# Dense products beside a column-tiled run, issued as four 128x32 column tiles

## The chip, the cores and the metric

The kernel runs on one core of one Trainium2 chip. The metric is the device time of one execution in microseconds. Matrix products run on TensorE (PE in the profile; its weight loads are PEld), the other work on VectorE (DVE), ScalarE (ACT) and GpSimd (POOL), and SyncE (SP) issues the transfers.

## The reference

One transformer block over 2048 tokens of width 1024: an attention with a memory that is carried over four segments of 512 tokens, with 32 heads of 32, and a gated feed-forward layer of width 3584. Cut to what matters:

```
h  = x + A(layernorm(x))        h2 = h + B(layernorm(h))

A: q, k, v = x @ wq, x @ wk, x @ wv          # heads of 32, 4 segments of 512
   for s in range(4):
       p     = softmax(qs @ ks.T * 32**-0.5 + causal mask)
       a_dot = p @ vs
       a_mem = (phi(qs) @ M) / (phi(qs) @ z + 1e-6)     # phi(t) = t+1 if t>0 else exp(t)
       o     = sigmoid(beta) * a_mem + (1 - sigmoid(beta)) * a_dot
       M, z  = M + phi(ks).T @ vs, z + sum(phi(ks))
   return o @ wo
B: return (silu(x @ w1) * (x @ w3)) @ w2
```

Weights and activations are bf16.

## The kernel before

Every piece of work is made into an operation of a graph (`Op`), with its engine, the buffers it reads and writes, the PSUM banks of its group, and a function `emit` that issues its instructions later. The order on each engine is not searched for: the table `ORDER` lists, for each of the five engines, the numbers of the operations in sequence, `BANKS` gives the PSUM bank of each group, and `HOLD` adds some waits between transfers and matmuls. `schedule` puts the operations in that order; its own model of times only decides the order in which the program is written down and which DMA semaphore is used. `Graph.emit` then walks through the operations, puts the waits on semaphores ahead of each, and calls its `emit`; the last instruction of an operation signals.

TensorE is used in four shapes, and each of its operations has a `mode`:

- "full", 128 rows by 128 columns: all dense products (the q, k, v projections, `wo`, and the feed-forward layer), made by `mms` (line 707 issues them), and the first transposes (line 719). `mms` cuts the eight products of a PSUM group into operations of four matmuls each, every one with its own weights of 128x128 and 512 moving columns.
- "row", 32 by 128: the scores of attention (line 1079), four heads at once in four row tiles, into banks 0 to 3.
- "col", 128 by 32: numerators and denominators of attention (`finish`, lines 1165 and 1172) and the memory's products (`products`, line 1000), four heads at once in four column tiles, each tile with weights of 32 columns.
- "tile", 32 by 32: the reading of the memory (line 1296).

There are eight half segments of attention, 0 to 370 us. In each, ten score operations alternate with dense operations that come from other parts of the model (projections of the next segment, `wo` of an earlier one, or the feed-forward layer), so that ScalarE has time for the exponentials. Then a column run follows: numerators, denominators, memory products. Ahead of it and behind it stand dense runs. After the last one the feed-forward layer is left, dense throughout.

## Time and profile before

| | |
|---|---|
| median of 3 runs (lowest to highest) | 884.22 us (883.82 to 886.32) |
| span of the profiled execution | 882.6 us (its time with what lies around the span is not given apart) |
| TensorE busy | 877.7 us, 5821 matmuls |
| weight loads | 398.1 us, 5821 |
| VectorE, ScalarE, GpSimd busy | 439.5, 301.7, 162.9 us |
| dense products of 512 columns (line 707), by the page's groups | 896 + 896 for w1 and w3, 952 for w2, 256 for wo, the rest projections |
| 128x32 matmuls of line 1172 and of line 1000 | 896 and 384 |
| granted TensorE clock | 1.000 |
| instruction packets of TensorE's queue | 46 |

How to read it: busy times of PE are unions of pipelined matmuls whose ends are modelled, so a matmul of 512 columns is listed with 379 ns although the next one starts sooner. The starts in the timeline are what counts. The forms read rows*columns of the array, then partitions x moving elements: 128*32 128x512 is one column tile. A window row lists, for each engine, busy time and count of instructions, then the granted clock, the DMA share and GB/s.

### The profile page before, as it was taken

The page shows a single profiled execution, that of the slowest core. Times are in us where ns is not written, and L with a number is a line of the kernel's source. Part 1 is how long each engine was busy: PE and PEld are TensorE (multiplying, and loading weights), DVE is VectorE, ACT ScalarE, POOL GpSimd, SP SyncE. Part 2 cuts the span into 40 slices and gives each one's busy share as a digit, 9 for nine tenths or more (in the row PEclk, how much of TensorE's full clock was granted, in tenths as well). Part 3 has the DMA queues.
Part 4 walks back from the last instruction along what each step waited for, and adds up shares of the span by engine and source line. Part 5 has one row for each costly group of instructions (what it writes and reads, how often), then busy time and mean ns, then how long its engine had stood idle before and what let it go on. Part 6 is the DMA issues. An engine that isn't in the chain of part 4 may idle for free.

```text
span 882.6 us, 13741 instructions
## 1 busy us (share of the span) xinstructions
PE 877.7 (99%) x5821; PEld 398.1 (45%) x5821; DVE 439.5 (50%) x735; ACT 301.7 (34%) x345; POOL 162.9 (18%) x226
## 2 busy tenths in 40 slices
PE   8999999999999999999999999999999999999998
PEld 5443444444444444444444444444444444444445
DVE  5787878876666777745354301322243344231011
ACT  5878675768656655511111000111011111110000
POOL 1534344335242444303000000000000000000000
PEclk9999999999999999999999999999999999999999
DMA  7989938555962627395483411211322322201011
GB/s 227 214 185 215 251 85 225 144 144 161 233 158 82 168 68 172 93 283 160 113 242 95 113 36 30 78 54 54 96 76 62 96 72 61 89 7 48 19 42 42
DMA packets 148956, 105.75 MB, mean 120 GB/s; under 512 B 46368, under 2 KB 134688, under 8 KB 147872
## 3 DMA queue, kind: packets, MB, share of 16 engines
q1 hardware_dynamic: 148896, 104.89, 45.8%
q8 instruction: 46, 0.75, 0.4%
q14 instruction: 14, 0.11, 0.0%
HBM read 84.94 MB, written 9.44 MB: 107 GB/s over the span
## 4 chain that ended last, share of the span: by engine, by line
PE 99%; DMA 1%; SPq 0%; issue 0%; DVE 0%; DVEq 0%
PE ps L707 92%; PE ps L1079 3%; PE ps L1172 3%; DMA wp<-in_A_wk_dram 1%; PE ps L1000 0%; PE ps L1296 0%; SPq L388 0%; PE ps L1165 0%; PE ps L719 0%; DVE ob L1401 0%; DVEq L524 0%
## 5 line engine op out<-in xcount | busy, mean ns | idle before, releaser
L707 PE MATMUL ps<-hnT,w1b 128*128 128x512 bf16 x896 | 216.2, 379 | 0.0
L707 PE MATMUL ps<-hnT,w3b 128*128 128x512 bf16 x896 | 213.9, 379 | 0.0
L707 PE MATMUL ps<-w2b,hm 128*128 128x512 bf16 (+2 forms) x952 | 199.2, 366 | 0.0
L1369 ACT ACTIVATE sg<-ps 128x512 bf16<-128x512 f32 x112 | 66.8, 597 | 385.5 <-PE ps L707 384.3
L1372 DVE SCALAR_TENSOR_TENSOR t<-sg,ps 128x512 bf16<-128x512 bf16 x112 | 76.6, 685 | 190.1 <-ACT sg L1369 189.8
L1093 ACT ACTIVATE et<-ps 128x2048 bf16<-128x2048 f32 x80 | 150.1, 1876 | 47.7 <-PE ps L1079 45.8
L707 PEld LDWEIGHTS ps<-w2b,hm 128*128 128x128 bf16 x952 | 90.9, 98 | 103.2 <-issue 0.3
L707 PEld LDWEIGHTS ps<-hnT,w1b 128*128 128x128 bf16 x896 | 86.3, 98 | 105.6 <-issue 5.6
L707 PEld LDWEIGHTS ps<-hnT,w3b 128*128 128x128 bf16 x896 | 86.4, 98 | 105.3 <-issue 3.1
L1102 POOL TENSOR_SCALAR_AFFINE_SELECT et<-et 128x512 bf16<-128x512 bf16 (+1 forms) x96 | 83.1, 877 | 112.5 <-ACT et L1093 112.5
L1377 DVE SCALAR_TENSOR_TENSOR hm<-t,ps 128x512 bf16<-128x512 bf16 x112 | 76.2, 684 | 42.5 <-PE ps L707 40.6
L1401 DVE TENSOR_TENSOR ob<-hr,ps 128x512 bf16<-128x512 bf16 (+2 forms) x34 | 21.9, 654 | 122.4 <-PE ps L707 122.3
L707 PE MATMUL ps<-xnT,wp 128*128 128x512 bf16 (+1 forms) x352 | 60.9, 321 | 1.1 <-DMA wp<-in_A_wk_dram 1.1
L707 PE MATMUL ps<-wo,oT 128*128 128x512 bf16 x256 | 61.1, 380 | 0.0
L707 PE MATMUL ps<-hnT,wp 128*128 128x512 bf16 x256 | 59.7, 380 | 0.0
L1118 DVE TENSOR_TENSOR sum<-sum,et 128x512 bf16<-128x512 bf16 (+1 forms) x64 | 40.5, 640 | 6.1 <-POOL et L1102 3.8
L707 PEld LDWEIGHTS ps<-xnT,wp 128*128 128x128 bf16 x352 | 27.9, 98 | 27.3 <-issue 3.5
L707 PEld LDWEIGHTS ps<-wo,oT 128*128 128x128 bf16 x256 | 23.8, 98 | 29.7 <-issue 3.0
L707 PEld LDWEIGHTS ps<-hnT,wp 128*128 128x128 bf16 x256 | 23.6, 98 | 29.7 <-issue 3.7
L1079 PE MATMUL ps<-qT,kT 32*128 32x128 bf16 (+3 forms) x512 | 31.7, 301 | 0.0
L1341 DVE TENSOR_TENSOR h<-h,ps 128x512 bf16<-128x512 bf16 x32 | 21.6, 679 | 20.2 <-PE ps L707 19.8
L707 PE MATMUL ps<-wp,hnT 128*128 128x512 bf16 x128 | 30.4, 380 | 0.0
(101 smaller groups left out, 568.2 us busy)
## 6 DMA issues: line engine op xcount, KB each, us to landing
w1b<-in_B_w_dram SPq DMA_DIRECT2D x28, 512.0 KB, 4.1
w3b<-in_B_w_dram SPq DMA_DIRECT2D x28, 512.0 KB, 4.4
wp<-in_A_wv_dram SPq DMA_DIRECT2D x8, 1024.0 KB, 5.9
wp<-in_A_wq_dram SPq DMA_DIRECT2D x7, 1024.0 KB, 6.2
wp<-in_A_wk_dram SPq DMA_DIRECT2D x7, 1024.0 KB, 7.6
w2b<-in_B_w_dram SPq DMA_DIRECT2D x7, 1024.0 KB, 5.8
h<-in_A_x_dram SPq DMA_DIRECT2D x16, 256.0 KB, 3.0
h_scr<-h SPq DMA_DIRECT2D x16, 256.0 KB, 3.3
```

What stands on the lines that cost most here:

```text
L707: return [e.matmul(p[0](gr), p[1], p[2], start=p[3], stop=p[4]) for p in part]
L1079: ins.append(e.matmul(self.bank(gr, j, 512 - 128 * kc, off), k[r, g0 + g, 128 * kc:128 * kc + 128], q[r, g0 + g, 128 * kc:512], start=True ...
L1093: return [e.activation(et[:, :, :], src, AF.Exp, scale=self.scale)]
L1102: self.pool_op(lambda e, v=v, pat=pat: e.affine_select(v, v, pattern=pat, compare_op=ALU.is_ge, fill=0.0, base=0, channel_multiplier=-1), ...
L1118: lambda e, gr: [e.tensor_tensor(o, a, b, op=ALU.add) for o, a, b in sums],
L1172: ins.append(e.matmul(self.ps[32 * i:32 * i + 32, b * 512 + c0:b * 512 + c0 + n], lhsT(i, kc, j), rhs(i, j), start=kc == 0 and j == first, ...
L1341: self.g.op("dve", dve_ns(512), lambda e, gr, hs=hs: [e.tensor_tensor(hs, hs, self.bank(gr), op=ALU.add)], reads=[hs], writes=[hs], cls=1, ...
L1369: self.g.op("act", act_ns(512), lambda e, gr, sg=sg: [e.activation(sg, self.bank(gr), AF.Tanh, scale=0.5)], writes=[sg], cls=0, group=gg)
L1372: e.scalar_tensor_tensor(t1, sg, 1.0, self.bank(gr), op0=ALU.add, op1=ALU.mult)], reads=[sg], writes=[t1], cls=0,
L1377: e.scalar_tensor_tensor(dst, t1, 0.5, self.bank(gr), op0=ALU.mult, op1=ALU.mult)], reads=[t1], writes=[dst], cls=0,
L1401: self.g.op("dve", dve_ns(n), lambda e, gr, hs=hs, ob=ob, n=n: [e.tensor_tensor(ob, hs, self.bank(gr, 0, n), op=ALU.add)], reads=[hs], wri ...
```

## The change

Dense operations of `mms` carry a mark `free`. After the order is fixed, `shape` goes through TensorE's list. For each unbroken run of free operations it looks at the modes of the two neighbours; if one of them is "col" and none is "full" (the ends of the list count as "full"), the whole run is given the mode "col". A dense operation in that mode issues each of its matmuls as four: tile j takes columns 32j to 32j+31 of the weights and writes partitions 32j to 32j+31 of the same PSUM bank, with the same 512 moving columns. All dense matmuls now set `stop`, in the manner of the column runs. Order, banks and waits are as before, and every operation signals once, with its last instruction.

```diff
+        self.shape(order["pe"])
...
+    def shape(self, pe):
+
+        i = 0
+        while i < len(pe):
+            j = i
+            while j < len(pe) and pe[j].free:
+                j += 1
+            sides = {pe[k].mode if 0 <= k < len(pe) else "full" for k in (i - 1, j)}
+            if "col" in sides and "full" not in sides:
+                for o in pe[i:j]:
+                    o.mode = "col"
+            i = j + 1
...
-            def emit(e, gr, part=part):
-                return [e.matmul(p[0](gr), p[1], p[2], start=p[3], stop=p[4]) for p in part]
-
             used = part if eager or i else items
-            last = self.g.op("pe", cost, emit, reads=[p[1] for p in used] + [p[2] for p in used],
+            last = self.g.op("pe", cost, None, reads=[p[1] for p in used] + [p[2] for p in used],
                              cls=cls, group=group)
-            last.mode = "full"
+            last.mode, last.free = "full", True
+
+            def emit(e, gr, part=part, op=last):
+                if op.mode == "full":
+                    return [e.matmul(p[0](gr), p[1], p[2], start=p[3], stop=True,
+                                     skip_group_check=True) for p in part]
+                return [e.matmul(p[0](gr)[32 * j:32 * j + 32, :], p[1][:, 32 * j:32 * j + 32], p[2],
+                                 start=p[3], stop=True, tile_position=(0, 32 * j),
+                                 skip_group_check=True) for p in part for j in range(4)]
+
+            last.emit = emit
```

## The prediction

> **What bounds the kernel now.** I read the page first (shares, chain, instruction queue), then the chain in order of time, the TensorE timeline around the places that change, stretches with their instruction counts, and the transfers in short stretches.

> ```profile
> span 882.6 us, 13741 instructions
> PE 877.7 (99%) x5821; PEld 398.1 (45%) x5821; DVE 439.5 (50%) x735; ACT 301.7 (34%) x345; POOL 162.9 (18%) x226
> q8 instruction: 46, 0.75, 0.4%
> PE 99%; DMA 1%; SPq 0%; issue 0%; DVE 0%; DVEq 0%
> PE ps L1000 <- issue: 0.3, 1, 0.3
> ```

> TensorE is the bound: it is busy for 99% of the span and carries 99% of the chain. So whatever a PE instruction gains or loses goes straight to the end. The last row is one of PE's three waits, and the only one that no engine or transfer explains. It becomes important below. The median of the runs is 884.2, so 1.6 us lie around the span of 882.6; I make the sum against the span and add it to 884.2.

> **What a matmul and a switch of tiling cost.** The chain gives whole dense runs, the timeline the borders (start, length, operation, count).

> ```profile
> 47.48 4.42 PE ps L707 x20
> 55.47 2.70 PE ps L707 x12
> 370.70 25.14 PE ps L707 x116
> 47.08 0.40 PE L1079 MATMUL ps<-qT,kT 32*128 32x128 bf16 x8
> 47.41 1.04 PE L707 MATMUL ps<-xnT,wp 128*128 128x512 bf16 x4
> 51.83 1.27 PE L1172 MATMUL ps<-et,v 128*32 128x512 bf16 x32
> 52.93 0.23 PE L1172 MATMUL ps<-et,ones 128*32 128x128 bf16 x4
> 54.76 0.71 PE L1172 MATMUL ps<-et,v 128*32 128x512 bf16 x16
> 55.41 0.39 PE L707 MATMUL ps<-wp,xnT 128*128 128x512 bf16 x1
> 221.30 2.36 PE L1172 MATMUL ps<-et,v 128*32 128x512 bf16 x64
> 223.59 1.04 PE L707 MATMUL ps<-wo,oT 128*128 128x512 bf16 x4
> 224.56 0.40 PE L1165 MATMUL ps<-pq,zsel 128*32 128x512 bf16 x4
> ```

> The 116 and the 20 matmuls each include one leaving price, so a dense matmul of 512 columns takes (25.14 - 4.42) / 96 = 0.2158 us. Then 20 of them should take 4.32 and take 4.42: leaving a dense run for a column run costs 0.10. Twelve should take 2.59 and take 2.70: 0.11 towards scores. Four take 0.97 (223.59 to 224.56) against 0.86: 0.11. Entering: the scores at 47.08 stream 128 + 384 columns (0.216) and the dense run starts 0.33 later: 0.11. The 16 numerator matmuls at 54.76 are four quads of 512 + 384 + 256 + 128 = 1280 columns (0.54) and the next run starts 0.65 later: 0.11. I take 0.107 per switch.

> **The change, part by part.** Counted from the timeline, 17 dense runs have a column run on at least one side and no full one: 8 lie row to column (20, 24, 20, 20, 16, 24, 20, 20 matmuls), 7 column to row (12, 8, 8, 8, 8, 8, 12), one column to column (4, at 223.59) and one column to block (116, at 370.63): 348 matmuls, 34 switches.

> 1. *Switches.* Each of the first 15 and the last keeps one switch (row to column, say) and loses one; the column-to-column run loses two: 16 + 2 = 18 removed, 18 x 0.107 = 1.9 us gained. No direct row-to-column step is in this trace. From below it could cost nothing (all 34 gone, 3.6 us); from above as much as both steps it replaces (only the 2 gone, 0.2 us). I take one ordinary switch, the value that entering, leaving, row and column all share.

> 2. *348 matmuls become 1392 column tiles.* The 32 numerators at 51.83 stream 2 x 1280 columns in quads, with new weights for every tile, in 1.10 us; at the dense rate they would take 1.08, and the first after any switch is some 0.01 slow. The 64 at 221.30 stream 5120 columns in 2.29, of which 0.11 is the switch: 2.18 against 2.16. So a quad costs 0 to 0.004 us more than the dense matmul, 0 to 1.4 us in all; I take 0, since about half of the excess of 0.02 is the switch's. The four weight loads of a quad are hidden: the next rows show loads and matmuls of columns keeping step at 10 ns each, and a converted quad has 216 ns for eight.

> 3. *Other engines.* The order and the waits stay. A column run that follows a dense one comes up to 0.1 earlier against exp, masks and evictions. PE has no wait there now; if one appeared it would eat at most that 0.1, 0.8 us for eight. Vector, scalar and GpSimd have half their time free. No data transfer is added.

> 4. *Instructions.* 348 x 3 more matmuls and as many loads: 2088 on 11,642. They have to be fetched. 11,642 plus about 200 waits of PE's own in 46 packets of 16 KB is 256 a packet, so 8 more packets. That is nothing for the queue, but when they arrive matters:

> ```profile
> 51.80:55.40 3.60, 3.60 (x177) 2.73 (x176) 2.79 (x9) 2.51 (x4) 0.00 (x0) 1.00 0.53 132
> 178.59 0.18 PE L1000 MATMUL ps<-v,pkn 128*32 128x33 bf16 x1
> 179.05 0.27 PE L1000 MATMUL ps<-v,pkn 128*32 128x33 bf16 x15 [0.28 <-issue]
> DMA  0090000000000000000000000000000000000000
> q8 instruction: 1, 0.02, 3.5%
> 0.00:178.60 178.60, 176.28 (x1738) 81.37 (x1739) 135.92 (x253) 124.45 (x127) 71.08 (x112) 1.00 0.78 191
> 0.00:52.98 52.98, 50.66 (x413) 25.66 (x417) 34.40 (x79) 35.03 (x44) 19.34 (x42) 1.00 0.84 224
> ```

> A column run of attention eats 353 instructions in 3.6 us, 10 ns each. In the one at 175 PE stands still at 178.59 for 0.46 - in the middle of a quad of one operation, so no wait of the program is there. The transfer row (176 to 178.6, 40 slices) shows a single instruction packet, in the third slice, at 176.2, on an otherwise idle queue. I read it so: instructions come in blocks of 256, two blocks are held, and when PE crosses into a block the one after it is fetched; here the block was used up in 2.73 us less the stall and the next came 2.9 us after its packet began (2.73 after the crossing at 176.32). The crossing points then are every 256 instructions from number 1738 + 1739 + 44 waits = 3521, so at 961 and so on.

> Now move them. Up to 47.4 nothing changes; then 20 converted matmuls add 120, and 413 + 417 + 11 waits + 120 = 961: a crossing now falls at 52.98, just into a column run, and the whole block is eaten inside it. Doing this for all crossings gives five tight ones; the others have 3.4 us or more, above the 2.73 and the 2.9, and those under 4.7 lie where the data queue is nearly idle. Before the change only two blocks fell so: that at 176.32, and one crossed at 278.59 with 2.43 us and no stall. Here is what each of the five has, and what the transfers do around them:

> ```profile
> 52.98:54.98 2.00, 2.00 (x141) 1.71 (x134) 1.25 (x3) 1.73 (x3) 0.00 (x0) 1.00 0.63 156
> 93.44:95.38 1.94, 1.94 (x140) 1.60 (x129) 0.46 (x1) 0.47 (x1) 0.00 (x0) 1.00 0.56 194
> 132.72:136.43 3.71, 3.71 (x122) 2.07 (x112) 2.47 (x6) 3.10 (x7) 0.75 (x3) 1.00 1.03 350
> 224.79:227.05 2.26, 2.26 (x121) 1.73 (x114) 1.39 (x4) 0.85 (x2) 0.00 (x0) 1.00 1.03 344
> 278.57:280.92 2.35, 2.35 (x129) 1.91 (x132) 0.89 (x3) 0.00 (x0) 0.00 (x0) 1.00 0.06 19
> ...
> DMA  1101010000000000000000000000000000000000
> DMA  1010010000000000000000000000000000000000
> ...
> q8 instruction: 1, 0.02, 1.7%
> q1 hardware_dynamic: 1631, 1.65, 101.2%
> q8 instruction: 1, 0.02, 1.2%
> q14 instruction: 1, 0.01, 0.5%
> q8 instruction: 1, 0.02, 20.5%
> ```

> Behind each stretch stands the time that the 256 instructions last after the change; the last number but one is the DMA share. The two rows of slices are 52.4 to 53.4 and 92.9 to 93.6: the data queue is all but empty at the crossings and its load begins behind them, so the idle answer of 2.73 holds and the stalls are 0.7 and 0.8. At 278.57 (share 0.06) 0.4; the last row is 278 to 278.3, the packet of the block without a stall: it began 0.3 before its crossing, and 2.8 was enough. At 224.79 the queue is full (1.03). The three rows with 1631 packets are 224.8 to 229.7 and have the instruction packet, which up to 229.5 is not there, though the crossing of before was at 225.2. So it starts at 229.6, is usable at 232.5 and is needed at 227.05: 5.4. At 132.72, share 1.03, the packet of before is in 132.7 to 136.3 (the row with 1.7%) and not in 132.7 to 136.1: usable at 139.1, needed at 136.43, 2.7. The long run at 370.63 has 6.7 to 6.9 us a block under full load, 0 to 1.3 of stall for each of three; I take 0. Stalls: 0.7 + 0.8 + 0.4 + 5.4 + 2.7 = 10.0, and the 0.46 of before goes, as its crossing moves away.

> Their bounds: from below 2.4 (the five at the idle answer: 0.7, 0.8, 0.4, 0.5 and 0) or nothing if my reading of one stall is wrong; from above, if at 52.98 and 93.44 too the packet falls behind the loads issued there, some 2.5 and 3.8 more, and 2 in the long run.

> [...]

> **Sum.** -1.9 (switches) + 0 (quads) + 10.0 - 0.5 (fetch) = +7.6: 884.2 + 7.6 = 891.8.

> **Rivals.**
> - *The fetch stays hidden.* Only the switches count: 882.3, within 0.3% of 884.2 (that bound, 2.65 us, is about what a measurement of this kernel tells from no change). For it: one stall of 0.46 in 46 fetches. Against it: that stall's place in the middle of a quad. With stalls at the lower bound of 2.4 it is 884.2, the same case.
> - *Faster: a direct step between tilings is free.* Its place is the 16 remaining switches; at 0 each all 34 go, 3.6 us: 880.6. It decides once 25 of 34 go and no block runs late. Against it: all kinds of switches cost alike.
> - *Quads cost more than shown*, 0.004 each, fetch hidden: 883.7, no change either.
> - *The clock falls in the long stalls.* The first products of the kernel run below full rate:

> ```profile
> L707 PE MATMUL ps<-oT 128*128 128x512 bf16 x13 | 5.7, 612 | 1.2 <-DVE oT L772 1.2
> ```

>   5.7 us for 13, 0.44 each, twice the 0.2158. If the 5.4 us of idling threw PE back to that for about as long, 2.8 us more: 894.6, and 897 were it to happen twice. The granted clock is 1.00 in every stretch quoted, but no stretch here idles that long. [...]

> **How the numbers follow.** Forecast with stalls that outweigh the gain 0.50, with the clock 0.08: slower 0.58. Fetch hidden or nearly so 0.30, dearer quads 0.05: same 0.35. Free step 0.07: faster. The range goes from all stalls absent (882) to the queued answers at the first two crossings (891.8 + 2.5 + 3.8 = 898.1): 882 to 898. Inside the forecast alone it is 887 to 898.

> **What would show it.** Instruction packets 54 instead of 46. Dense groups at L707 split, 348 fewer of 128*128 and 1392 of 128*32, with starts of quads 216 ns apart. No 0.1 before the column runs, one 0.107 where row meets column. PE waits put down to issue, of 0.7 to 5.4 us, near 54.9, 95.3, 136, 227 and 281, none near 178.6; DMA and other engines as before. The prediction is wrong if such waits are missing, if the quads are not 216 ns apart, or if a direct switch costs much less or more than 0.107.

## The result, and the profile after

The changed kernel takes 895.62 us (894.01 to 899.67, four executions), the kernel before, measured beside it on the same chip, 884.25. The ratio is 1.0126, with an interval of 1.0099 to 1.0153: slower, as forecast (891.8, range 882 to 898). The profiled execution is the longest of the four, 899.67 with a span of 898.0; its span is 15.4 above the 882.6 of before, and the account below is made for it.

The page of the changed kernel: span, TensorE's busy time, its instruction packets, and the engines' shares of the chain.

```profile
span 898.0 us, 15748 instructions
PE 877.5 (98%) x6784; PEld 405.3 (45%) x6865; DVE 439.7 (49%) x735; ACT 302.1 (34%) x345; POOL 163.1 (18%) x226
q8 instruction: 54, 0.88, 0.4%
PE 97%; issue 2%; DMA 1%; SPq 0%; DVE 0%; ACT 0%; ACTq 0%; DVEq 0%
```

TensorE was busy 877.7 us before and is 877.5 now (some 2 more, were all its products on record): what grew is mostly the time in which TensorE waits. 54 packets instead of 46 stand there, and "issue", 0% of the chain before, has 2%. (6865 loads with 6784 matmuls: 81 matmul records are missing, all of them at line 728.)

TensorE's waits: place, what released it, us in total, times, the longest. Line 730 issues the column tiles, 728 the products that stayed dense, 1194 numerators and denominators.

```profile
PE ps L730 <- issue: 5.2, 2, 3.1
PE ps L728 <- issue: 4.9, 15, 2.5
PE ps L728 <- DMA wp<-in_A_wk_dram: 2.5, 1, 2.5
PE ps L1194 <- issue: 0.5, 1, 0.5
```

Of the 15 at line 728 one is a wait, of 2.5; the other 14, of 0.17 each on average, stand where a matmul is missing from the records. So there are four waits for "issue" of half a microsecond or more. The timeline has their places (start, length, operation, count; the idle time ahead stands in brackets, measured from the modelled ends):

```profile
57.62 0.54 PE L1194 MATMUL ps<-et,v 128*32 128x512 bf16 x6
58.70 0.45 PE L1194 MATMUL ps<-et,v 128*32 128x384 bf16 x8 [0.54 <-issue]
...
98.79 0.38 PE L730 MATMUL ps<-wp,hnT 128*32 128x512 bf16 x2
101.23 2.35 PE L730 MATMUL ps<-wp,hnT 128*32 128x512 bf16 x30 [2.06 <-issue]
...
143.45 0.59 PE L728 MATMUL ps<-hnT,wp 128*128 128x512 bf16 x2 [0.16 <-issue]
146.56 1.98 PE L728 MATMUL ps<-hnT,wp 128*128 128x512 bf16 x5 [2.52 <-issue]
...
236.63 1.46 PE L730 MATMUL ps<-wo,oT 128*32 128x512 bf16 x21
241.19 0.83 PE L730 MATMUL ps<-wo,oT 128*32 128x512 bf16 x11 [3.11 <-issue]
```

Three of the four lie inside a quad, four column tiles that run together (0.2158 us for the four, below): two of its tiles or one are issued, and the rest comes 0.9 to 3.5 us later. The one at 143 stands behind the third of the four products of a dense operation (one of the three is missing from the records). No semaphore of the program stands at these places. By the starts, less the time that the product under way takes anyway (0.216 for 512 columns), TensorE stands idle for 0.70, 2.23, 2.68 and 3.27; with 0.22 at 408.96 in the long run that is 9.1 us. Where a quad is split, the tiles that come late stream their columns alone, 0.16 to 0.22 more; that is 0.8 for the four split quads, the one at 408.96 with them. The weight loads are all on record, and between the four waits there are 509, 505 and 1013 of them; with as many products that is 1018, 1010 and 2026 instructions, and with TensorE's own 7, 14 and 21 waits on semaphores 1025, 1024 and 2047: 4, 4 and 8 blocks of 256. In the transfers from 235 to 238 there is no instruction packet (first row below), in those from 238 to 240 there is one, ahead of the restart at 241.19, with the data queue full in both:

```profile
q1 hardware_dynamic: 1000, 1.01, 99.7%
...
q1 hardware_dynamic: 613, 0.63, 97.1%
q8 instruction: 1, 0.02, 3.6%
```

The granted clock fell as well, in four of the five stretches below; the last numbers of a row are clock, DMA share, GB/s.

```profile
10.00:13.80 3.80, 3.78 (x39) 3.79 (x40) 0.88 (x3) 1.50 (x4) 0.00 (x0) 0.55 1.01 270
102.40:105.90 3.50, 3.17 (x22) 1.01 (x16) 0.57 (x1) 1.72 (x1) 1.27 (x1) 0.52 1.11 257
106.00:109.00 3.00, 3.00 (x21) 1.21 (x20) 1.89 (x3) 1.46 (x3) 0.00 (x0) 1.00 1.05 184
147.00:150.00 3.00, 3.00 (x8) 0.88 (x6) 2.25 (x3) 0.00 (x0) 1.04 (x1) 0.50 0.04 13
242.40:245.80 3.40, 3.29 (x8) 1.21 (x8) 1.31 (x2) 2.92 (x3) 0.00 (x0) 0.51 0.19 42
```

Behind each of the three longer waits TensorE ran at half clock for 3.41 us (from 106 on it is full again). By the starts of the same instructions in both kernels this cost 1.6, 1.6 and 1.7. The stretch at 10 to 13.8, and the wait of 2.5 for `wk` ahead of it (1.1 before), need no change of the kernel: up to 47 us both issue the same instructions, and of 19 executions of the kernel before in one sitting 14 had a mean clock of 1.000, 13 of them with 883.9 to 884.7 us, and five had 0.998 with 886.3 to 886.5. One stretch of 3.4 us at half clock is 0.5 x 3.4 / 885 = 0.002 of the mean, which fits one in each of these five. In the profiled run it took 1.6 and the longer wait 1.5.

The account: -1.9 (switches) - 0.5 (the wait at 178.59, which is gone) + 9.1 (waits for instructions) + 0.8 (split quads) + 4.9 (half clock behind the waits) + 3.0 (start) = 15.4, against 15.4.

Last, the price of switches and quads, in the long run. Row tiles, then dense products as column tiles (eight for `w1`, twelve for `w3`), then numerators:

```profile
377.72 0.40 PE L1101 MATMUL ps<-qT,kT 32*128 32x128 bf16 x8
378.05 1.91 PE L730 MATMUL ps<-hnT,w1b 128*32 128x512 bf16 x32
379.78 2.76 PE L730 MATMUL ps<-hnT,w3b 128*32 128x512 bf16 x48
382.37 1.48 PE L1194 MATMUL ps<-et,v 128*32 128x512 bf16 x36
```

Twelve quads last from 379.78 to 382.37: 2.59, or 0.2158 each, the dense rate, and the numerators follow without a step. The scores stream 512 columns (0.216), the first quad starts 0.33 behind them: 0.11 for the direct switch from rows to columns.

### The profile page after: what moved, and what is told of

It reads as the page before. It is cut to its first block, busy times and chain, and to the rows that moved or that the text cites. A ratio compares the mean times of both kernels' runs of the same rounds, so it can differ in the third digit from the quotient of the medians.

```text
span 898.0 us, 15748 instructions
## 1 busy us (share of the span) xinstructions
PE 877.5 (98%) x6784; PEld 405.3 (45%) x6865; DVE 439.7 (49%) x735; ACT 302.1 (34%) x345; POOL 163.1 (18%) x226
## 4 chain that ended last, share of the span: by engine, by line
PE 97%; issue 2%; DMA 1%; SPq 0%; DVE 0%; ACT 0%; ACTq 0%; DVEq 0%
PE ps L728 82%; PE ps L730 8%; PE ps L1101 3%; PE ps L1194 3%; DMA wp<-in_A_wk_dram 1%; PE ps L1022 0%; SPq L389 0%; PE ps L1318 0%; PE ps L741 0%; PE ps L1187 0%; DVE t L1394 0%; DVE hm L1399 0%; ACT sg L1391 0%; DVE ob L1423 0%; DVE lnst L856 0%
## 5 line engine op out<-in xcount | busy, mean ns | idle before, releaser
L728 PE MATMUL ps<-hnT,w1b 128*128 128x512 bf16 x788 | 192.3, 379 | 1.2 <-issue 0.5
L728 PE MATMUL ps<-hnT,w3b 128*128 128x512 bf16 x784 | 189.4, 379 | 1.4 <-issue 0.3
L728 PEld LDWEIGHTS ps<-hnT,w1b 128*128 128x128 bf16 x804 | 77.7, 98 | 94.9 <-issue 4.8
L728 PEld LDWEIGHTS ps<-hnT,w3b 128*128 128x128 bf16 x804 | 77.5, 98 | 94.6 <-issue 3.1
L728 PE MATMUL ps<-xnT,wp 128*128 128x512 bf16 (+1 forms) x323 | 55.7, 323 | 3.0 <-DMA wp<-in_A_wk_dram 2.5
L728 PE MATMUL ps<-wo,oT 128*128 128x512 bf16 x221 | 54.2, 383 | 0.5 <-issue 0.2
L728 PE MATMUL ps<-hnT,wp 128*128 128x512 bf16 x189 | 45.6, 384 | 3.4 <-issue 3.3
L728 PEld LDWEIGHTS ps<-wo,oT 128*128 128x128 bf16 x228 | 21.4, 98 | 26.9 <-issue 2.9
L728 PEld LDWEIGHTS ps<-hnT,wp 128*128 128x128 bf16 x196 | 18.0, 98 | 25.8 <-issue 6.6
```

Source lines behind the costliest of these rows:

```text
L728: return [e.matmul(p[0](gr), p[1], p[2], start=p[3], stop=True, skip_group_check=True) for p in part]
```

## The experiments

The theory, the author's reading of these traces: TensorE holds two blocks of 256 instructions (5821 loads, 5821 products and 201 waits of the kernel before came in 46 packets, 6865, 6865 and 201 now in 54, some 258 a packet; and the wait at 178.59 stood 256 instructions behind 176.32, where one packet had just started); a crossing into a new block starts the packet of the one after it, which stands behind data loads in the queue (none from 235 to 238, with the data queue at 99.7%); a block used up before the packet has landed makes TensorE wait (0.70 to 3.27 so far), and the longer waits bring the half clock (2.23, 2.68 and 3.27 did, 0.70 did not). The rivals: column tiles themselves are slow; TensorE takes this many instructions only so fast, loads or no loads; the program waits for something not seen.

**As many instructions, no column tiles.** Converted products are issued as four dense pieces of 128 moving columns.

```diff
-    e.matmul(p[0](gr)[32 * j:32 * j + 32, :], p[1][:, 32 * j:32 * j + 32], p[2], ...
-             tile_position=(0, 32 * j), ...) for p in part for j in range(4)
+    e.matmul(p[0](gr)[:, 128 * j:128 * j + 128], p[1],
+             p[2][:, 128 * j:128 * j + 128], ...) for p in part for j in range(4)
```

> The 348 dense products that the change turns into column tiles are issued here as four pieces along the moving columns (128x128 weights, 128 columns each): as many instructions at the same places as the changed kernel, but no column tiling and all 34 switches back. Theory (late instruction blocks): the stalls of the changed kernel stand at about the same places (near 98, 144 and 238 us, 2 to 3.5 each, with the half clock behind each), 54 instruction packets, and the time is that of the changed kernel plus 1.9 for the switches plus 348 x 0.009 = 3.0 for the smaller pieces (4 x 56 against 216 ns): about 900 us (896 to 904). Rival (the column tiles themselves, their weights or their mixing with other shapes, cost the time): no stalls, 884.2 + 3.0 = 887 us.

Measured: 899.33 (896.81 to 901.34), ratio 1.016 (1.0135 to 1.0185), beside 884.36 for before. Its waits, and twelve products in pieces in the long run:

```profile
PE ps L730 <- issue: 4.3, 2, 2.6
PE ps L728 <- issue: 4.4, 16, 1.8
...
376.10 2.84 PE L730 MATMUL ps<-hnT,w3b 128*128 128x128 bf16 x48
378.87 2.36 PE L1194 MATMUL ps<-et,v 128*32 128x512 bf16 x64
```

Waits of 0.63, 1.92, 2.01 and 2.74 stand at 56.4, 97.9, 141.1 and 233.9, near the same instructions as in the changed kernel, with none of the dense products in column tiles: the tiles are not the cause, the number of instructions is. That it is slower still has two reasons: all 34 switches are paid (1.9), and by these rows a product in four dense pieces takes (2.77 - 0.11) / 12 = 0.222 instead of 0.2158, some 2 us over 348. Four column tiles, at 0.2158 a product, were the cheaper way to cut it.

**The same kernel, fewer bytes in the queue.** In the changed kernel, and in the kernel before, the 21 loads of 1 MB behind the first three projection weights shrink to 16 KB. Order, waits and all instructions of TensorE stay; the products use what their buffers held before, so the output is not the model's.

```diff
-    self.g.dma(w[:, :, :], src, cls=1)
+    self.g.dma(w[:, :, :], src, cls=1).emit = lambda e, g, w=w, src=src: [
+        e.dma_start(w[:, 0:1, 0:64], src[:, 0:1, 0:64])]
```

> The changed kernel with every 1 MB load of projection weights behind the first three cut to 16 KB (21 loads; the products then use what the buffer held before, so the output is not the reference's). Nothing on TensorE's side changes. Theory (the size of a stall is set by the loads ahead of the instruction packet): the blocks still start at 54, 94, 133 and 226, but the packets now find a short queue, so the stalls come to the idle answer: 0.7 near 55 to 57, 0.8 near 96 to 99 (up to 1.5, since the four loads of the output weights there stay), 0 near 136 to 144, 0.5 near 227 to 238; sum 2.0 to 2.7 instead of 8.9, and no half clock behind them: 0 to 1 us above the kernel before with the same loads cut, about 883 to 886. Rival (PE takes that many instructions only so fast, whatever the loads): the stalls keep 0.7, 2.2, 2.7 and 3.3 with the half clocks, and the time stays 9 to 12 above the kernel before with the same loads cut, 892 to 896.

> The kernel before with the same 21 loads cut to 16 KB, the baseline for that run (the output is not the reference's). TensorE waits for none of these loads once it has started, so both theories expect 882 to 884.5; the stall of 0.46 near 178.6, on an idle queue, stays.

Measured: the changed kernel 885.88 (884.78 to 889.53), ratio to the unaltered kernel before 1.0018 (1.0005 to 1.0031); the kernel before with the cut 884.61 (883.54 to 886.87), 0.9997 (0.9984 to 1.001). Packets, waits, and one stretch (132 to 146) of the changed kernel with the cut, then the same stretch of the changed kernel without it:

```profile
q8 instruction: 54, 0.88, 0.4%
PE ps L730 <- issue: 1.2, 2, 0.8
PE ps L1194 <- issue: 0.6, 1, 0.6
132.00:146.00 14.00, 14.00 (x301) 7.26 (x290) 8.97 (x17) 9.72 (x15) 6.43 (x9) 1.00 0.09 24
```

```profile
132.00:146.00 14.00, 11.89 (x310) 6.56 (x310) 7.86 (x17) 9.55 (x15) 5.66 (x9) 1.00 0.62 197
```

The same 54 packets and the same tight blocks, but the DMA share falls from 0.62 to 0.09, and TensorE is busy for all of 14.00 us. By the starts the waits are 0.76 at 57, 1.02 at 98, 0.30 at 230 and 0.50 at 396, 2.6 in all, and no half clock stands behind any. The trace has the start of every packet. Take the crossing as the place 256 instructions ahead of each of the changed kernel's four waits, at 55.9, 97.0, 140.1 and 235.4. There the packets start 0.6, 1.3, 4.0 and 3.5 us behind the crossing; at the same instructions with the loads cut it is 0.5, 0.2, 1.0 and 0.0. Where TensorE waited for one of them, it went on 2.2 to 3.0 us behind the packet's start, with the loads and without. The 1.26% that the change costs become 0.18%: some 9.7 of 11.4 us go with the loads. This is the experiment that decides: a tight block alone cost 1.02 us at most here, what made it 2.2 to 3.3 us is the load traffic ahead of its packet.

The kernel before with the cut missed one point of its expectation: the wait near 178.6 was to stay, and it is not there. Its packet starts at 176.53, TensorE had the next block by 179.0, and the products run through:

```profile
179.07 0.27 PE L1000 MATMUL ps<-v,pkn 128*32 128x33 bf16 x16
```

So that wait of 0.46, on which the prediction built its reading, comes and goes between executions on an idle queue; that it is also missing where blocks were moved (below) shows nothing by itself. Between the pair 1.3 us are left; the terms are -1.9 (switches) + 2.6 (waits) + 0.8 (the quads that they split) = 1.5. The profiled pair differs at the start too (a wait of 2.3 against 1.7 and a stretch of low clock).

**Only the two loads at the longest wait.** In the changed kernel the two 1 MB loads ahead of 238 are cut in the same way.

```diff
+    if (s, kind, half) in ((3, "v", 1), (3, "k", 1)):
+        self.g.dma(w[:, 0:1, 0:64], src[:, 0:1, 0:64], cls=1)
```

> The changed kernel without most of the last loads of wv and wk (2 MB that are on their way when PE stalls at 238 us; 16 KB of each are left, so the last half of k and v is made with old weights). Theory (the block is late because its packet queues behind data): the stall of 3.3 us at 238 falls to under 1 and the half clock behind it goes, the stalls at 98 and 144 stay: 5 us less than the changed kernel, about 890.5. Rival (the block is late whatever the queue holds, or the stall is no fetch): the stall at 238 stays at 3 us, 895.5.

Measured: 891.54 (888.5 to 900.34), 1.0087 (1.0061 to 1.0114), close to what was expected, and in the profiled execution the wait near 238 is gone. But that execution is the longest of ten, 900.34, and a wait that was not touched has grown to 4.5, at 101.3:

```profile
PE ps L730 <- issue: 4.5, 1, 4.5
```

Up to there the program is that of the changed kernel, where this wait was 2.23; one near 57, 0.70 there, is 1.6 here. So the waits at one and the same block differ between executions by 2 us and more, which fits the wide spread of these kernels' times.

**Two tiles or two halves instead of four.** 696 additional instructions instead of 2088: as two column tiles 128*64 (`range(2)`, 64 in place of 32), and as two dense halves of 256 moving columns.

```diff
-    ... p[1][:, 32 * j:32 * j + 32], p[2], ... tile_position=(0, 32 * j) ... for j in range(4)
+    ... p[1][:, 64 * j:64 * j + 64], p[2], ... tile_position=(0, 64 * j) ... for j in range(2)
```

> The changed kernel with each converted product as two column tiles 128*64 instead of four 128*32: 696 instructions more than before instead of 2088, so a block of 256 lasts 13.8 us inside a converted run instead of 6.9. Fetch theory: the crossings that fall into a block shorter than 2.8 us are then two, near 94.8 (1.8 us long, 0.5 to 2.2 us of stall, depending on the loads ahead of the packet) and near 179 (2.6 us, 0 to 0.3), with perhaps 0 to 1.5 near 133 (3.1 us under full load); the stalls near 57, 143 and 238 are gone, 49 instruction packets. If a step from 128*64 tiles to 128*32 or 32*128 ones is one switch, as from the dense ones, and the step between 128*64 and a column run is free, 15 to 18 switches of 0.107 go: 884.3 - 1.9 + 1 to 3 = 883.5 to 886. If a step between the two widths of column tiles costs a switch, the gain is gone: 885.3 to 887.5. Rival (column tiles as such cost, not their number): pairs start later than 216 ns, and the kernel stays above 890.

> The same number and place of instructions as with two tiles of 64, but each converted product is two full 128*128 matmuls of 256 moving columns, so no switch of tiling goes. Fetch theory: the same stalls at the same places (near 94.8, perhaps 133 and 179), 1 to 3 us, all 34 switches paid: 885.3 to 887.5, and the difference to the two tiles of 64 is what the removed switches are worth, 1.9 us if the two widths of column tiles join freely, 0 if not. Rival (a dense product in pieces is itself slower): pieces start later than 108 ns apart.

Measured: 888.15 (885.36 to 890.13), 1.0034 (1.002 to 1.0047), and 887.82 (886.11 to 891.7), 1.0045 (1.0027 to 1.0063), beside 884.6. In the profiled executions, which are the shortest of each kernel, the waits near 57, 98, 143 and 238 are gone, and the expected ones near 94.8, 133 and 179 are under 0.3; one of 0.6 and 1.1 that the profile puts down to issue stands near 297, ahead of the reading of the memory, where no block is short, and is not explained. A third of the instructions, about a third of the loss. Whether the two widths of column tiles join freely, the timeline of the tiles of 64 tells:

```profile
48.95 1.03 PE L730 MATMUL ps<-xnT,wp 128*64 128x512 bf16 x8
49.81 1.89 PE L730 MATMUL ps<-wp,xnT 128*64 128x512 bf16 x16
51.63 1.27 PE L1194 MATMUL ps<-et,v 128*32 128x512 bf16 x32
```

Eight products in pairs take 1.73 and the numerators start 1.82 behind them: 0.09, a switch. So nothing is gained with tiles of 64, and the two kernels come out alike. Both medians lie somewhat above their expectation (885.3 to 887.5), 2 to 3 above the profiled executions; the median executions were not profiled, and what they wait for is not known.

**Moving the crossings.** Four kernels only shift where the blocks begin: more, shorter warm-up matmuls in the kernel before (+176 instructions) and in the changed one (+204), or the first products of the first projection cut in four (+48 in the kernel before, +60 in the changed one).

```diff
-    self.warm(12)
+    self.warm(100, cols=61)      # kernel before; changed kernel: warm(114, cols=54)
...
+    n = 4 if k < cut else 1      # the first 8 (before) or 10 (changed) products
```

> The kernel before, with its 12 warm-up products of 512 columns at the start cut into 100 of 61 columns: as many columns, 176 instructions more, nothing else changed. Theory (late blocks): the crossings move back by 176 instructions into column runs; by the crossing times of the kernel before, blocks last 2.3, 2.6 and 3.6 us at 52, 92 and 222 us with a full data queue, so stalls of about 3.6, 3.3 and 2.3 us there, the half clock behind each (1.8 more), none at 178.6: 884.2 + 9 + 5 - 0.5 = 898 us (891 to 902). Rival (the column tiles cost the time) or instruction fetch is of no account: 884 us, at most 0.5 more at the start.

> The changed kernel, with its warm-up cut into 114 products of 54 columns: 204 instructions more at the start. Theory (late blocks): the crossings move to where the shortest block is 2.4 to 2.9 us on an idle queue and 4.8 to 5.2 on a full one; stalls of 0.3 to 1.1 each, 4 us in all, too short for the half clock: 884.2 - 1.9 - 0.5 + 4 = 886 us (883 to 891). Rival (the column tiles cost the time): 895.6 us as before the shift.

> The kernel before, with the first 8 dense products of the first projection (at about 15 us, long before the first column run) issued in four pieces of 128 columns: 48 instructions more, 8 x 0.009 = 0.07 us of work, no column tile added, the start as before. From the traces so far: a packet waits for the loads issued more than about 1 us ahead of the crossing, 4 to 5 us at most, else it starts within 0.3 of it, and its instructions are usable 2.5 after its start. Theory (late blocks): crossings move back by 48; the blocks crossed into at 93.7 and 132.2 us last 4.9 and 3.5 us there with loads just issued: stalls of 1.3 and 2.4, the half clock behind the longer one (1.8), none at 178.6: 884.4 + 5 = 889.5 us (886.5 to 893). Rival (column tiles cost the time, or fetch is of no account): 884.4 us.

> The changed kernel, with 10 dense products of the first projection issued in four pieces, 60 instructions more at about 15 us. Theory (late blocks), by the same rule: the crossings near 52.1, 92.4 and 132.2 us come ahead of the loads there; stalls of 0.9, 1.1 and 0.2, too short for the half clock, and none of 3 us at 238: 884.4 - 1.9 - 0.5 + 2.1 = 884 us (882.5 to 887), 11 us under the changed kernel. Rival (column tiles cost the time): 895.6 us.

Measured: the kernel before with +176: 887.6 (886.24 to 889.41), 1.0029 (1.0017 to 1.0041); the changed one with +204: 895.88 (892.47 to 897.01), 1.0116 (1.0091 to 1.0141); the kernel before with +48: 888.01 (885.33 to 890.55), 1.0027 (1.0012 to 1.0041); the changed one with +60: 891.67 (887.09 to 894.54), 1.0065 (1.004 to 1.009). A wait row of each of the first three (two of the second), and the longest wait of the fourth with the stretch behind it:

```profile
PE ps L1000 <- issue: 0.6, 1, 0.6
```

```profile
PE ps L730 <- issue: 6.5, 2, 3.4
PE ps L1194 <- issue: 1.6, 2, 0.9
```

```profile
PE ps L1091 <- issue: 1.6, 1, 1.6
```

```profile
137.28 1.47 PE L739 MATMUL ps<-hnT,wp 128*32 128x512 bf16 x22 [2.67 <-issue]
136.50:141.00 4.50, 3.72 (x36) 1.57 (x37) 1.12 (x3) 2.46 (x2) 0.69 (x2) 1.00 0.63 212
```

The waits do move with the blocks: with +204 those at 98.8, 143.7 and 237.7 are gone and others stand at 55.3, 59.1, 102.8, 241.5 and 293.9 (1.1, 3.3, 3.6, 1.0 and 0.9); the kernel before loses its wait at 178.6 and gets others. That fits the fetch theory. But of the times that I had worked out for chosen shifts three were missed: 898 and 886 for the first two, 884 for the fourth. The third came out within its range (889.5, 886.5 to 893), but only 2.4 above the 885.57 of the kernel before beside it where 5 had been expected, with one wait of 1.6 and no half clock behind it in place of two waits and a half clock. With +176 the queue had just run empty at the crossings that I had counted on, with +204 new loads were issued just ahead of them. The expectations failed in that they fixed the load traffic at each crossing to a microsecond, and it is not fixed to that.

**Only the runs that should cost nothing.** Four of the 17 runs (the first, third, fourth and ninth) stay dense, with 6 more instructions at the start.

```diff
+    if n not in SKIP:            # SKIP = (0, 2, 3, 8)
         for o in pe[i:j]:
             o.mode = "col"
```

> Thirteen of the 17 runs are turned into column tiles (not the 1st, 3rd, 4th and 9th of them), and one dense product of the first projection is issued in four pieces (6 instructions): the choice for which the rule above leaves no block late. Theory: no stall near 55, 98, 136, 178.6 or 238 us, 14 switches of 0.107 gone and the 0.46 of before: 884.4 - 1.5 - 0.5 = 882.4 us (882 to 884). Rival (column tiles cost the time): 13 of 17 runs, 276 of 348 products, would leave about 893 us.

Measured: 889.12 (886.55 to 891.69), 1.0042 (1.0026 to 1.0058), another miss. The row is its longest wait for instructions, at 98.3:

```profile
PE ps L738 <- issue: 1.5, 1, 1.5
```

Waits of 1.6, 0.6, 0.5 and 0.4 are left, more than the 1.5 that 13 runs save (14 switches). The gain is spread over 18 places of 0.1, and one late packet takes more than all that a choice of runs leaves of it. No version here beat the kernel before.

## Why the prediction was right, and where it was off

1. *Switches*, -1.9. Confirmed by the trace: a direct step from rows to columns takes 0.10 to 0.11, and none is left between a converted run and a column run. The rival of a free direct step fell.
2. *Quads at no extra cost.* Confirmed, 0.2158 each. Taking 0 out of 0 to 1.4 was right, and the rival of dear quads fell.
3. *Instructions*, +10.0. The reading of the waits agrees with the runs (54 packets; waits in the middle of quads; loads cut, waits shrunk from 0.70, 2.23, 2.68 and 3.27 to 0.76, 1.02, none and 0.30), the sum measured 9.1, and 0.8 more for the split quads, which it left out. Term by term: at the block of 52.98 0.70 for 0.7; at 132.72 2.68 for 2.7; at 278.57 none for 0.4; at 224.79 3.27 for 5.4; at 93.44 2.23 for 0.8; in the long run 0.22 for 0. The term for 93.44 is the upper bound's case in a smaller size: its packet did fall behind loads issued around the crossing, and with the loads cut it is 1.0. The term for 224.79 was too long: its packet was taken to start where that of a different block had started, 4.8 behind the crossing, and to be usable 2.9 later; it started 3.5 behind and TensorE went on 2.3 later. Both errors come mainly from a start read off one trace for a moment that shifts; that they cancel is luck. That the waits can be as small as the lower bound's 0.7, 0.8, 0.4, 0.5 is shown by the run with cut loads: 0.76, 1.02, none and 0.30. The stall at 178.59 itself was a weak footing: the kernel before with cut loads does not have it.
4. *The clock* is the step that failed. The rival "the clock falls in the long stalls" had 0.08 and was the case: it names the wait of 5.4 alone, and waits of 2.23, 2.68 and 3.27 brought the fall, for 4.9 us in the profiled execution. The four executions have mean clocks of 0.992, 0.994, 0.996 and 0.998, by 0.002 a stretch four, three, two and one. With two or three stretches of 1.6 to 1.7 the median of 895.6 comes down to 891 to 892, where the sum without a fall of the clock, 891.8, had it. The price in that rival (2.8 a fall) was too high, as these falls lasted 3.4 us and not as long as the wait; their number was too low.
5. *Other engines* hid what they were said to hide: outside of the start, no wait of over 0.2 on VectorE, ScalarE or a load came up in the changed kernel.

## What to carry to other kernels

Count the instructions per microsecond, not only the cycles: cutting products into tiles that ran as fast (0.2158 us a quad) lost 1.26% here, where a block of 256 instructions was used up in some 2 to 4 us (55.9 to 57.8, 140.1 to 143.7) and loads stood in the queue. Look for such waits in the middle of one operation, released by "issue", and test them by shrinking the loads while TensorE's instructions stay. A gain of 0.1 at each of 18 places is less than one wait of 2.2 us with the low clock behind it, and moving the instructions about to dodge it cannot be planned from one trace.

## What the runs showed of the hardware that was not expected

- In these traces it was how a wait lay on a grid that told whether the half clock came behind it, and not its length alone. In each trace the stretches of half clock begin and end on a grid of 3.413 us; those of the changed kernel that begin at 10.38, 102.54, 146.92 and 242.49 lie 27, 13 and 28 steps apart. Up to the last product, the clock fell behind 14 steps in the thirteen traces, and in each of these TensorE had stood idle, by the starts and counting gaps of 0.15 us or more, for 2.03 us or longer. In no other step at full clock was it idle for more than 1.99. Two rows of the changed kernel, a step of the wait at 237.7 and the step behind it, then the two steps of the wait at 134.2 of the kernel with +60:

```profile
239.08:242.49 3.41, 1.16 (x15) 0.44 (x17) 1.04 (x2) 0.09 (x1) 0.57 (x2) 1.00 1.28 199
242.49:245.90 3.41, 3.39 (x8) 1.21 (x8) 1.31 (x2) 2.93 (x3) 0.00 (x0) 0.50 0.19 42
...
132.98:136.39 3.41, 1.64 (x98) 1.03 (x86) 2.36 (x6) 2.03 (x5) 0.64 (x3) 1.00 1.03 355
136.40:139.81 3.41, 2.53 (x30) 1.05 (x31) 0.31 (x1) 1.27 (x2) 0.79 (x2) 1.00 0.85 286
```

The waits of 2.23, 2.68 and 3.27 (changed kernel), 2.74 (dense pieces), 3.55 (+204), 2.28 and 4.65 (two loads cut) put at least 2.09 into one step. Those of 1.92 and 2.01 (dense pieces), 2.83 (+60) and 3.32 (+204) did not: a border cuts the longer three in two, 0.25 and 1.76, 1.94 and 0.89, 1.72 and 1.59. A fall lasted one step, or two where TensorE idled again for 1 us or more in the first (behind 3.55 and 4.65). So in these runs the border lay at about 2 us of idling in a step; 1.99 and 2.03 are too near to each other to give it more exactly.
